# Storing dV and dK from the ScalarE queue, one head later, instead of from the GpSimd queue

## The chip, the cores and the metric

One core of a Trainium2 chip runs the whole kernel. The metric is the device time of that core in microseconds (us), as a median over several executions. Every profile quoted here is of one execution. Two executions of one kernel on different chips or in different rounds differ by up to 0.9% (1738.99 to 1753.90 us for the kernel before), so small differences are judged by ratios against the kernel before, run in the same rounds on the same chip.

## The reference

The program is forward and backward of one decode step: layer norm, attention of one query row against a cache of 4096 keys (4 batches, 32 heads, head size 128), layer norm, SwiGLU. What matters here is the size of two gradients, those of the two caches:

```python
k_cache, v_cache: [4, 32, 4096, 128] bf16          # 128 heads of 1 MB each
dV[b, h] = outer(p, dO)                            # p: [4096], dO: [128]
dP       = V @ dO
dS       = p * (dP - c) * scale
dK[b, h] = outer(dS, q)
```

Each is an outer product, trivial to compute, and 134 MB to write.

## The kernel before

A first loop over 128 heads reads K and V (268 MB). A middle part does the small matrices. The second loop, which the change touches, reads V again (1 MB a head), transposes it on TensorE, computes dP, and builds dV (`gv`) and dK (`gk`) on VectorE, 1 MB each, which are then stored.

All large tiles live in 22 slots of one pool. `give()` puts a slot at the end of a queue of free slots; a later tile takes the oldest, and its writer waits until the slot's last user (often a store) is done.

```python
def front(s):                       # one head ahead of back()
    ...                             # now and then: replicate rows (ScalarE copies)
    V_T(s, psT)                     # PE transposes V; 4 ScalarE copies of 128x1024 to VT
    ...                             # 32 matmuls: dP_ps
    VTs.pop(s).give()
    ...                             # P2: a small copy on GpSimd

def back(s):
    gv = Slot("gv")
    outer(gv.heads(), P2, reps["rdo", ...])                           # VectorE
    nc.gpsimd.dma_start(out=rows_of(out_3[b, h]), in_=gv.heads())     # store dV
    gv.give()
    ...                                                               # dS on VectorE
    gk = Slot("gk")
    outer(gk.heads(), dS2, reps["rq", ...])                           # VectorE
    nc.gpsimd.dma_start(out=rows_of(out_2[b, h]), in_=gk.heads())     # store dK
    gk.give()

def prefetch(s):
    while nv["next"] < min(NH, s + 7) and len(free) > 5:
        load_V2()                   # SP issues the load of a later V

prefetch(0)
front(0)
for s in range(NH):
    prefetch(s + 1)
    ...
    front(s + 1)
    back(s)
    step("s", ...)                  # a piece of side work: weight gradients, dx, ...
```

## Time and profile before

| | before |
|---|---|
| time, median of the runs before the prediction | 1743.91 us (1738.99 to 1747.68) |
| DMA bytes | 707.86 MB, mean 406 GB/s |
| busy share of the span: PE, DVE, ACT, POOL | 76%, 72%, 55%, 28% |
| second loop | about 720 us to the end |

The prediction shows the lines and how they are read. Its DMA row gives the busy share of the 16 DMA engines in tenths, for 40 equal slices of the span.

### The profile page before, as it was taken

What the parts mean: (1) busy time and instruction counts of PE and PEld (TensorE: products, weight loads), DVE (VectorE), ACT (ScalarE), POOL (GpSimd) and SP (SyncE); (2) the same over time, 40 slices, a digit from 0 to 9 for tenths busy, and PEclk for the clock granted to TensorE, in tenths of its full rate; (3) what the DMA queues carried; (4) which work ended last, traced back from release to release, by engine and by line L of the source; (5) the groups of instructions that cost most, each with busy time, mean ns of one, the idle gap of its engine ahead of it and who ended that gap; (6) DMA issues with size and microseconds to landing.
All of it is one profiled execution on the core that took longest, in us unless ns stands there. A gap on an engine that the chain in (4) does not pass through costs nothing.

```text
span 1743.7 us, 44065 instructions
## 1 busy us (share of the span) xinstructions
PE 1324.2 (76%) x18993; PEld 1122.6 (64%) x18993; DVE 1251.9 (72%) x1382; ACT 956.4 (55%) x1463; POOL 491.6 (28%) x804
## 2 busy tenths in 40 slices
PE   5889888888888888888877876676667766786653
PEld 4777766666666667878777875565446555665553
DVE  5899899899898996567746765647545555655674
ACT  3455445445444444665555655575566666766653
POOL 2333333333333331213321331212212212322332
PEclk8999999999999999755555555666556555656555
DMA  9999999999999999899999999999999999999997
GB/s 397 410 418 419 419 418 419 419 416 418 410 413 397 418 405 362 320 403 411 423 418 419 417 417 417 417 420 387 423 412 403 415 420 393 386 415 412 416 415 301
DMA packets 107124, 707.86 MB, mean 406 GB/s; under 512 B 11233, under 2 KB 18921, under 8 KB 23985
## 3 DMA queue, kind: packets, MB, share of 16 engines
q1 hardware_dynamic: 67280, 422.68, 59.5%
q0 software_dynamic: 39648, 282.36, 39.3%
q8 instruction: 149, 2.44, 0.5%
q14 instruction: 47, 0.38, 0.1%
HBM read 422.58 MB, written 282.34 MB: 404 GB/s over the span
## 4 chain that ended last, share of the span: by engine, by line
DMA 38%; DVE 11%; issue 6%; PE 4%; ACT 2%; POOL 1%; DVEq 0%; POOLq 0%; ACTq 0%; SPq 0%
DMA out_dram<-gk 21%; DMA out_dram<-gv 11%; DVE gk L1077 4%; DVE gv L1077 4%; DMA out_dram<-gw 4%; DMA out_dram<-gwq 1%; ACT VT L740 1%; POOL P L1073 1%; DMA V<-in_A_v_cache_dram 1%; PE pt_tps L739 1%; PE M_ps L436 1%; DVE PK L421 1%; ACT wo L216 0%; DVE dS L1095 0%; PE pt_w L564 0%
## 5 line engine op out<-in xcount | busy, mean ns | idle before, releaser
L740 ACT COPY VT<-pt_tps 128x1024 bf16<-128x1024 bf16 x512 | 492.8, 1015 | 286.9 <-PE pt_tps L739 121.8
L739 PE MATMUL pt_tps<-ident_b,V 128*128 128x128 bf16 x4096 | 457.7, 296 | 168.3 <-ACT VT L740 165.1
L739 PEld LDWEIGHTS <-V 128*128 128x128 bf16 x4096 | 407.0, 139 | 237.2 <-issue 224.7
L1077 DVE TENSOR_TENSOR gv<-P,reps 128x4096 bf16<-128x4096 bf16 x128 | 293.0, 2289 | 256.4 <-DMA out_dram<-gk 145.6
L1077 DVE TENSOR_TENSOR gk<-dS,reps 128x4096 bf16<-128x4096 bf16 x128 | 293.4, 2292 | 76.7 <-DMA out_dram<-gv 34.9
L421 DVE TENSOR_TENSOR PK<-Kn,PK 128x4096 bf16<-128x4096 bf16 x128 | 302.9, 2367 | 36.4 <-POOL PK L417 36.4
L436 PE MATMUL M_ps<-PK,Vn 128*128 128x130 bf16 x4096 | 287.2, 223 | 43.2 <-DMA Vn<-in_A_v_cache_dram 43.0
L436 PEld LDWEIGHTS <-Vn 128*128 128x128 bf16 x4096 | 254.3, 99 | 63.1 <-DMA Vn<-in_A_v_cache_dram 53.6
L328 DVE STREAM_TRANSPOSE KT<-Kn 128x512 f32<-128x512 f32 (+1 forms) x321 | 251.0, 798 | 0.5 <-issue 0.5
L323 ACT COPY KT<-pt_tps 128x1024 bf16<-128x1024 bf16 x128 | 129.5, 1012 | 190.1 <-PE pt_tps L322 157.9
L1070 PE MATMUL dP_ps<-dOT_bf,VT 128*128 128x1 bf16 x4096 | 151.5, 166 | 72.7 <-ACT VT L740 62.7
L1070 PEld LDWEIGHTS <-VT 128*128 128x128 bf16 x4096 | 141.6, 104 | 84.6 <-ACT VT L740 73.9
L1099 POOL DMA_DIRECT2D out_dram<-gk x128 | 68.4, 534 | 383.7 <-DVE gk L1077 369.1
L1089 POOL DMA_DIRECT2D out_dram<-gv x128 | 68.7, 537 | 351.4 <-DVE dSt L1092 340.6
L417 POOL COPY PK<-P_all 128x64 bf16<-128x64 bf16 x128 | 32.5, 254 | 437.9 <-ACT P_all L411 432.6
L336 POOL COPY zq<-qT_bf 128x2 bf16<-128x2 bf16 x128 | 152.3, 1190 | 0.0
L1073 POOL COPY P<-P_all 128x64 bf16<-128x64 bf16 x128 | 121.5, 949 | 0.0
L411 ACT COPY P_all<-pt_P 32x64 bf16<-32x64 bf16 x256 | 52.1, 203 | 58.2 <-PE pt_P L407 56.0
L322 PE MATMUL pt_tps<-ident_b,Kn 128*128 128x128 bf16 x1024 | 80.5, 223 | 0.7 <-DVE qrep L282 0.7
L446 PE MATMUL kP_ps<-PK,onesw 128*32 128x512 bf16 x1024 | 80.1, 389 | 0.0
L322 PEld LDWEIGHTS <-Kn 128*128 128x128 bf16 x1024 | 62.1, 100 | 26.3 <-issue 26.3
L400 ACT ACTIVATE Pn<-E,rl 128x1024 bf16<-128x1024 f32 x64 | 73.7, 1151 | 2.8 <-DVE rl L397 2.8
(234 smaller groups left out, 1298.2 us busy)
## 6 DMA issues: line engine op xcount, KB each, us to landing
Kn<-in_A_k_cache_dram SPq DMA_DIRECT2D x128, 1024.0 KB, 14.3
Vn<-in_A_v_cache_dram SPq DMA_DIRECT2D x128, 1024.0 KB, 15.1
V<-in_A_v_cache_dram SPq DMA_DIRECT2D x128, 1024.0 KB, 11.4
out_dram<-gv POOLq DMA_DIRECT2D x128, 1024.0 KB, 19.3
out_dram<-gk POOLq DMA_DIRECT2D x128, 1024.0 KB, 19.8
wq<-in_A_wq_dram SPq DMA_DIRECT2D x8, 1024.0 KB, 11.2
out_dram<-gw POOLq DMA_DIRECT2D x6, 896.0 KB, 21.9
wo<-in_A_wo_dram SPq DMA_DIRECT2D x4, 1024.0 KB, 11.1
```

What stands on the lines that cost most here:

```text
L322: nc.tensor.transpose(pt[:, i, :], Kn[:, c * GW + i, :], ident_b[:])
L323: nc.scalar.copy(out=KT[:, c * GW:(c + 1) * GW, :], in_=pt[:])
L328: nc.vector.transpose(out=KT[:, c * w_:(c + n) * w_], in_=Kn[:, c * w_:(c + n) * w_])
L336: nc.gpsimd.tensor_copy(out=zq[gi % 2][hl][:, 32:132:67], in_=qT_bf[:, s:s + 1].to_broadcast([P, 2]))
L421: nc.vector.tensor_tensor(out=PK[:, :, 0:Dh].rearrange("p j (r t) -> p j r t", t=2), in0=Ks[s].heads().rearrange("p j (r t) -> p j r t", t=2),
L436: nc.tensor.matmul(hold["M"][:], lhsT=Vn[:, j, :], rhs=PK[:, j, :], start=(j == 0), stop=(j == SJ - 1))
L446: nc.tensor.matmul(hold["kP"][32 * q:32 * (q + 1), :, :], lhsT=ones_window(w), rhs=PK[:, j0:j0 + 4, 0:Dh], start=(w == 0 and c == 0), stop ...
L739: nc.tensor.transpose(pt[:, i, :], Vn[:, g * GW + i, :], ident_b[:])
L740: nc.scalar.copy(out=VT[:, g * GW:(g + 1) * GW, :], in_=pt[:])
L1070: nc.tensor.matmul(dP_ps[:, j:j + 1], lhsT=VT[:, j, :], rhs=dOT_bf[:, s:s + 1], start=True, stop=True)
L1073: nc.gpsimd.tensor_copy(out=P2[:], in_=P_all[:, s, :, None].to_broadcast([P, SJ, 2]))
L1077: nc.vector.tensor_tensor(out=dst.rearrange("p j (r t) -> p j r t", t=2), in0=col2[:, :, None, :].to_broadcast([P, SJ, Dh // 2, 2]), in1=r ...
```

## The change

Its intent is to take the stores' issue off GpSimd, and to keep ScalarE, which runs its instructions in order, from waiting for VectorE: the store of head s-1 is put behind ScalarE's copies for head s+1, when its data has long been made.

```diff
             outer(gv.heads(), P2, reps["rdo", s // REP][:, s % REP, :])
-            nc.gpsimd.dma_start(out=rows_of(out_3[b, h]), in_=gv.heads())
-            gv.give()
 ...
             outer(gk.heads(), dS2, reps["rq", s // REP][:, s % REP, :])
-            nc.gpsimd.dma_start(out=rows_of(out_2[b, h]), in_=gk.heads())
-            gk.give()
+            late.append((b, h, gv, gk))
+
+        late = deque()
+
+        def store_late():
+            b, h, gv, gk = late.popleft()
+            for out_ap, sl in ((out_3, gv), (out_2, gk)):
+                nc.scalar.dma_start(out=rows_of(out_ap[b, h]), in_=sl.heads())
+                sl.give()
 ...
                 front(s + 1)
+            if late:
+                store_late()
             back(s)
             step("s", 1 if s < 44 else 2 + (s % 4 == 0))
+        store_late()
         step("s", 400)
```

## The prediction

> **What bounds the kernel now.** I read the page's slices first, then the queue table, the windows of 50 us, and the chain of waits. The slices:
>
> ```profile
> DMA  9999999999999999899999999999999999999997
> GB/s 397 410 418 419 419 418 419 419 416 418 410 413 397 418 405 362 320 403 411 423 418 419 417 417 417 417 420 387 423 412 403 415 420 393 386 415 412 416 415 301
> ...
> q1 hardware_dynamic: 67280, 422.68, 59.5%
> q0 software_dynamic: 39648, 282.36, 39.3%
> ```
>
> The 16 DMA engines are busy in every slice but the seventeenth and the last, at 410 to 420 GB/s. The two queues fill 98.8% of their time. Both queues cost alike: 59.5/422.68 = 0.141% a MB for loads through the hardware queue, 39.3/282.36 = 0.139% for stores through the software queue; in the packet records an 8 KB packet takes 309 ns at the median in both. 707.86 MB at the 419 GB/s of the best long stretch is 1689 us, so whatever a change does to queues can gain at most 55 us (3.1%), and only where the engines are not yet full. The windows (us; busy us of PE, PEld, DVE, ACT, POOL; clock; DMA share; GB/s) say where that is:
>
> ```profile
> 720.00:725.00 5.00, 3.99 (x69) 3.57 (x67) 1.66 (x3) 3.85 (x4) 0.63 (x1) 0.80 0.51 206
> 725.00:730.00 5.00, 3.48 (x61) 3.12 (x58) 4.66 (x4) 3.76 (x4) 2.25 (x2) 0.88 0.30 126
> 730.00:735.00 5.00, 4.70 (x59) 4.45 (x58) 4.88 (x4) 3.36 (x4) 2.53 (x4) 0.50 0.95 387
> ...
> 950.00:1000.00 50.00, 42.75 (x529) 40.21 (x528) 38.41 (x32) 30.77 (x34) 16.91 (x24) 0.57 1.01 418
> ...
> 1500.00:1550.00 50.00, 41.44 (x526) 34.39 (x524) 37.36 (x31) 37.80 (x48) 18.62 (x23) 0.57 0.96 386
> ...
> 1728.00:1730.00 2.00, 0.00 (x0) 0.00 (x0) 0.00 (x0) 0.00 (x0) 0.00 (x0) 0.50 0.91 381
> ...
> 1732.00:1734.00 2.00, 0.00 (x0) 0.00 (x0) 0.00 (x0) 0.00 (x0) 0.00 (x0) 0.50 0.13 53
> ...
> 1738.00:1740.00 2.00, 0.00 (x0) 0.00 (x0) 0.00 (x0) 0.00 (x0) 0.00 (x0) 0.50 0.05 20
> ```
>
> The stage that the change touches, the second loop over 128 heads, runs from about 720 us to the end, at a share of 1.01 nearly throughout. It isn't full at its start (720 to 730), where few transfers are ready, a little around 1500, and in the last 8 us, where a share of 0.05 to 0.13 means that one or two of 16 engines still drain. The waits (us in total, times, longest) agree:
>
> ```profile
> DVE gv L1077 <- DMA out_dram<-gk: 145.6, 38, 9.9
> ...
> ACT VT L740 <- DMA out_dram<-gk: 64.7, 16, 12.4
> DVE gv L1077 <- DMA out_dram<-gv: 63.4, 22, 7.8
> ```
>
> The page's costliest groups and its table of issues have the stores themselves:
>
> ```profile
> L1089 POOL DMA_DIRECT2D out_dram<-gv x128 | 68.7, 537 | 351.4 <-DVE dSt L1092 340.6
> ...
> out_dram<-gk POOLq DMA_DIRECT2D x128, 1024.0 KB, 19.8
> ```
>
> VectorE and ScalarE wait for slots that a store still holds. A store of 1 MB lands 19.8 us after its issue, though at 419 GB/s it needs 2.5 us alone: it stands behind some seven others. So these waits are back-pressure of full DMA engines, not the cost of issuing. A head has 3 x 1.049 = 3.15 MB, 7.6 us at 415 GB/s (8.0 us with the weights and their gradients, estimated from the stage: (1743.7 - 720)/128); its other work is shorter: VectorE 2.29 + 2.29 + 0.25 + 0.23 = 5.1 us, ScalarE 4 x 1.015 + 0.3 = 4.4 us.
>
> **What the Trainium skill says.** Page "DMA: Bandwidth & Descriptors", section "Issuing engines are not separate DMA queues": transfers from the scalar, sync and gpsimd engines run on the same 16 engines and interleave, and several issuers save only issue time. The trace agrees (0.141 against 0.139% a MB). Same page, "SWDGE vs HWDGE vs iDMA": GpSimd's descriptors are built by software into rings in SBUF, from which VectorE can lock it out; transfers of SP and ACT are immune. The trace shows GpSimd's small copy of P at 0.25 us in places and 1.48 us beside VectorE's long multiply, but its issue at a steady 0.53 us, so I see no cost in the issue. Same page, "Latency and other measured facts": DMA engines 7 and 15 are usually slower, perhaps for the software rings. The trace does not name engines, but a transfer's completion semaphore rises 16 times, once per engine: for stores late in the kernel (1550 to 1700 us) the 16th rise comes 6 to 8 us after the 15th, for loads within 0.5 us. One engine lags in the software queue.
>
> **The change, part by part.**
> 1. Issue leaves GpSimd: 128 x (537 + 534 ns) = 137 us of 492 busy. GpSimd is idle 72% of the span, so nothing on the path: 0 us.
> 2. Issue comes to ScalarE. A 1 MB load takes SP 0.33 us to issue (the trace, typical); I take that for ACT: 2 x 0.33 = 0.66 us a head, 84 us in all. ScalarE goes from 4.4 to 5.0 us a head against 8.0 us: hidden, 0 us. The built program puts the two stores after the four VT copies of the head after next; their data was made an iteration before, so ScalarE rarely waits for VectorE.
> 3. The slots are held one head longer. I listed the slot order of both programs: before, a gv most often takes the slot of the gk stored three iterations before; after, gk most often takes that of a gv whose store is issued two iterations before, for the same head, three back. Loads still run seven heads ahead. So a cycle of three heads, 3 x 8.0 = 24 us, has to hold a store's flight, 2.3 us of multiply and up to one ScalarE turn of 5 us. That leaves some 17 us; the shortest flight of a store in 1000 to 1300 us was 9.2 us, with loads beside it. DMA stays full.
> 4. A new coupling: before, SP's loads have eight completion semaphores and GpSimd's stores eight more. In the changed program loads and stores share eight in rotation: each transfer must wait for the one eight places earlier, a store for one some three heads back. Eight MB in flight is 8.4/0.415 = 20 us of work. That is enough to keep the engines full, and the slot of point 3 waits for a younger store, so it binds first: I take 0 us in the plain stretch and +3 us where side work (small transfers, 1050, 1200, 1500 us) breaks the order.
> 5. The start. Before, stores 0 are issued at 721.6 and 727.8 us. After, both follow ScalarE's copies for head 2, which ended at 735.5. In 720 to 735 the engines moved 5 x (206 + 126 + 387) = 3.6 MB; with under 1 MB of late loads taken off, about 2.8 MB of stores move later: 2.8/0.415 = 7 us, and DMA time lost in a full stage does not come back: +7 us.
> 6. The end. The lagging engine drains alone for some 8 us. If hardware descriptors make it as even as loads are, part of that goes. Loads of the first loop still show two halves of engines 2 to 5 us apart, so I take half: -4 us. The last stores are issued 2.5 us or so later at most, behind a backlog of 20 us: 0.
> Sum: 1743.9 + 7 + 3 - 4 = 1749.9 us.
>
> **Rivals.** *(a) ScalarE becomes the bottleneck*: its order now ties copies, gradient evacuation and stores together; a store that waits for its semaphore stops the copies, PE, and dP. For it: ACT is 76% busy in 1500 to 1550, and one SP issue behind many small packets took 14 us. Against: 3 us spare a head, and older stores than those VectorE waits for. If 3 us in a third of the heads were lost: +120 us, 1870; half a us a head: +64 us. *(b) The software queue is the hidden brake*: rings and the lagging engine cost rate all along, and the store's wait for its slowest engine is what VectorE waits for. For it: the lag of 6 to 8 us of a 19 us flight. Against: the share is 1.01 and packets cost 309 ns in both queues, so the other engines weren't idle for it. At most the 55 us above; I'd expect 15 to 25 if true, 1720 to 1730. *(c) Nothing moves*: start and end cancel, 1740 to 1746.
>
> **Range and chances.** Runs of before span 1739 to 1748. Rival (c) and my sum lie within 10 us; (b) pulls down by 20, the mild form of (a) up by 25: 1732 to 1775. Over 2% faster (under 1709) needs nearly all of the 55 us: 0.04. Over 2% slower (above 1779) needs the strong form of (a), which I can't exclude as the coupling is new: 0.12. Within: 0.84.
>
> **What would show it.** Right: DMA share 1.01 at about 415 GB/s between 750 and 1700; an empty stretch of DMA until about 735 us; ScalarE's issue near 0.33 us; waits of VectorE for stores much as before; a shorter thin tail with the 16th rise close to the 15th. Wrong: DMA shares under 0.97 over long stretches, with ScalarE waiting for stores or loads just ahead of its issue (a), or above 420 GB/s throughout (b); an issue on ScalarE that lasts microseconds would sink point 2, loads landing much later than 11 us point 4.

## The result, and the profile after

The changed kernel takes 1748.82 us (median of six runs, 1746.28 to 1750.50); the kernel before took 1745.8 us with the new runs added (six, 1738.99 to 1748.95). The ratio is 1.002 with a 95% interval of 0.9997 to 1.0043: the same, perhaps slower by 3 us. Ratios here are the mean time of one kernel's fast runs over that of the other's of the same rounds, so they aren't quite the ratio of the quoted medians. A second job gave 1.0042 (1.0030 to 1.0055): on that chip the changed kernel is slower by 7 us.

From the page of the changed kernel, the DMA rows, the queues, and the two stores among the issues (KB each, median us from issue to landing):

```profile
DMA  9999999999999999599999999999999999999998
GB/s 398 410 418 418 419 418 418 419 413 418 417 415 398 418 406 360 245 397 412 423 419 397 423 419 414 409 397 387 425 425 415 414 412 410 414 419 415 418 424 337
...
q1 hardware_dynamic: 67280, 422.68, 59.5%
q10 hardware_dynamic: 36864, 268.45, 37.2%
q0 software_dynamic: 2784, 13.91, 2.0%
...
out_dram<-gv ACTq DMA_DIRECT2D x128, 1024.0 KB, 12.7
out_dram<-gk ACTq DMA_DIRECT2D x128, 1024.0 KB, 15.2
```

The stores have moved to a queue of their own, q10, and cost there what they did in q0: 37.2/268.45 = 0.139% of the engines' time for each MB. The DMA row is as full as before, with two differences: the seventeenth slice, the start of the second loop, falls from 8 to 5 tenths and from 320 to 245 GB/s, and the last one rises from 7 to 8. The stores land in 13 to 15 us instead of 19 to 20, so less stands in front of them, but that speeds nothing: the engines had work either way.

The windows of the start and of the end, from the changed kernel (us; busy us of PE, PEld, DVE, ACT, POOL; clock; DMA share; GB/s):

```profile
715.00:720.00 5.00, 3.99 (x33) 3.36 (x31) 2.58 (x2) 3.06 (x5) 3.41 (x5) 0.50 0.42 172
720.00:725.00 5.00, 4.29 (x63) 3.98 (x61) 1.79 (x3) 3.48 (x5) 0.00 (x0) 0.50 0.01 3
725.00:730.00 5.00, 4.36 (x70) 4.08 (x70) 4.05 (x5) 3.17 (x4) 0.24 (x1) 0.84 0.00 0
730.00:735.00 5.00, 3.93 (x55) 3.66 (x53) 2.66 (x2) 3.49 (x4) 0.00 (x0) 0.50 0.33 133
735.00:740.00 5.00, 4.65 (x58) 4.34 (x58) 4.83 (x5) 3.52 (x4) 0.24 (x1) 0.50 0.70 290
...
1736.00:1738.00 2.00, 0.00 (x0) 0.00 (x0) 0.00 (x0) 0.00 (x0) 0.00 (x0) 0.50 0.16 66
1738.00:1740.00 2.00, 0.00 (x0) 0.00 (x0) 0.00 (x0) 0.00 (x0) 0.00 (x0) 0.50 0.06 25
1740.00:1742.00 2.00, 0.00 (x0) 0.00 (x0) 0.00 (x0) 0.00 (x0) 0.00 (x0) 0.50 0.07 29
```

From 720 to 730 us the DMA engines do next to nothing, and from 715 to 740 they are never full. The end still has its thin tail: one of 16 engines (a share of 0.06) drains alone for several microseconds, although no large store goes through the software queue any more.

ScalarE's issues in order of time show why the start is empty. It is the timeline of ScalarE in the changed kernel (start, us, instruction; in brackets the idle time before and its releaser):

```profile
729.64 1.93 ACT L740 COPY VT<-pt_tps 128x1024 bf16<-128x1024 bf16 x2 [1.64 <-PE pt_tps L739]
731.75 1.93 ACT L740 COPY VT<-pt_tps 128x1024 bf16<-128x1024 bf16 x2 [0.18 <-PE pt_tps L739]
732.72 0.37 ACTq L1105 DMA_DIRECT2D out_dram<-gv  x1
733.19 0.38 ACTq L1105 DMA_DIRECT2D out_dram<-gk  x1
736.29 1.93 ACT L740 COPY VT<-pt_tps 128x1024 bf16<-128x1024 bf16 x2 [2.62 <-PE pt_tps L739]
738.41 1.93 ACT L740 COPY VT<-pt_tps 128x1024 bf16<-128x1024 bf16 x2 [0.19 <-PE pt_tps L739]
739.38 0.34 ACTq L1105 DMA_DIRECT2D out_dram<-gv  x1
```

The first stores leave behind the copies of head 2, at 732.7 us, though VectorE had made the first gv by 719.7; before the change they left at 721.5 and 727.7. The next pair follows one turn of ScalarE later, 6.7 us after the first.

**A ledger of idle time.** To add up where time went I summed the packet records of each trace: for a stretch, its length less the sum of its packets' times over 16. Records overlap a little (hence shares of 1.01), so a full stretch comes out slightly negative; only differences count. "Packets" is the sum of all packet times over 16, "end" is the time from the last packet to the end of the span. Each row adds up to its span. The lines r1 to r10 belong to the experiments below; r10 and r1 are second traces of the kernel before and of the changed one.

```
us              0-715  715-760  760-1040  1040-1600  1600-1720  1720-last  packets   end    span
before           -1.9     6.4     -2.9      -1.8       -1.4        7.7     1733.6    4.1   1743.7
before (r10)     -3.4     8.9     -2.7       0.2       -1.4        7.4     1732.3    4.1   1745.5
changed          -4.0    17.9     -1.7      -4.7       -0.8        6.2     1730.2    1.5   1744.6
changed (r1)     -3.5    18.4     -2.7      -1.9       -0.9        6.1     1731.0    1.5   1747.9
r2 late, GpSimd  -2.6     8.9     -3.1      -6.0       -1.4        9.8     1727.7    4.1   1737.4
r3 at once, ACT  -3.8    10.0     -2.4       3.8       -1.4        2.7     1728.5    1.5   1738.9
r4 first 3 once  -3.1    13.3     -2.8      -3.1       -0.8        5.2     1735.9    1.4   1746.0
r5 switch at 24  -3.2     6.8     -3.1      -2.0       -0.3        5.4     1731.5    1.5   1736.6
r6 two late      -3.1    24.2     -2.5      -1.0       -1.2        2.4     1731.8    1.5   1752.0
r7 early V       -3.6    13.3      5.5      -2.2       -1.4        4.6     1737.3    1.4   1754.9
r8 early V, Gp   -3.0     9.6     -2.4      -6.0       -1.4        9.4     1727.7    4.1   1738.1
r9 before copies -3.0    12.0     -2.4       2.6       -0.6        3.2     1730.6    1.4   1743.9
```

Two traces of one kernel agree within 1 to 3 us in each column. With the means of both traces, the change adds 10.5 us at the start (7.65 to 18.15) and takes away 2.5 in the stretch with side work, 1.4 in the tail, 2.4 in packet time, 2.6 at the end and 1.1 ahead of the stage (which is scatter, the program is the same there); it adds about 0.6 in each of the two other stretches. The sum is +1.7 us, the difference of the spans of these traces. The term of the side work is no larger than the scatter between two traces of one kernel there (2.0 and 2.8 us), so that part of what gives time back is not sure.

### The profile page after: what moved, and what is told of

Same layout as the page of the kernel before. It is cut to its first block, busy times and chain, and to the rows that moved or that the text cites. A ratio compares the mean times of both kernels' runs of the same rounds, so it can differ in the third digit from the quotient of the medians.

```text
span 1744.6 us, 43821 instructions
## 1 busy us (share of the span) xinstructions
PE 1316.6 (75%) x18993; PEld 1106.4 (63%) x18993; DVE 1253.4 (72%) x1382; ACT 956.8 (55%) x1463; POOL 291.2 (17%) x548
## 3 DMA queue, kind: packets, MB, share of 16 engines
q10 hardware_dynamic: 36864, 268.45, 37.2%
## 4 chain that ended last, share of the span: by engine, by line
DMA 34%; PE 10%; ACT 9%; DVE 6%; issue 3%; ACTq 1%; SPq 0%; POOL 0%; DVEq 0%
DMA out_dram<-gv 13%; DMA out_dram<-gk 10%; ACT VT L740 8%; DMA V<-in_A_v_cache_dram 7%; PE pt_tps L739 4%; DVE gv L1077 3%; DVE gk L1077 1%; DMA wq<-in_A_wq_dram 1%; PE dq_ps L902 1%; DMA w2a<-in_B_w_dram 1%; DMA w<-in_B_w_dram 1%; ACTq L1105 1%; PE dP_ps L1070 1%; DMA wo<-in_A_wo_dram 1%; PE rep_ps L1054 1%
## 5 line engine op out<-in xcount | busy, mean ns | idle before, releaser
L739 PE MATMUL pt_tps<-ident_b,V 128*128 128x128 bf16 x4096 | 446.1, 290 | 96.9 <-ACT VT L740 96.9
L739 PEld LDWEIGHTS <-V 128*128 128x128 bf16 x4096 | 396.2, 137 | 184.1 <-issue 176.6
L1073 POOL COPY P<-P_all 128x64 bf16<-128x64 bf16 x128 | 57.7, 466 | 587.0 <-DVE gv L1077 587.0
L1090 DVE TENSOR_SCALAR dSt<-dP_ps,c_rep 128x32 f32<-128x32 f32 x128 | 31.6, 247 | 79.2 <-PE dP_ps L1070 79.0
L1057 ACT CAST reps<-rep_ps 128x512 bf16<-128x512 f32 x64 | 37.4, 585 | 69.4 <-PE rep_ps L1054 50.6
```

The source lines that it names most:

```text
L739: nc.tensor.transpose(pt[:, i, :], Vn[:, g * GW + i, :], ident_b[:])
```

## The experiments

Theory S: the start alone costs, because ScalarE's place in the order delays the first stores while the DMA engines have nothing else; the rest gives a little back. Rival A: ScalarE becomes the bound. Rival C: the eight completion semaphores, which loads and stores now share, cost time. Rival N: there is no difference at all.

**r1, the changed kernel again** (no edit), in one job with r2, r3 and r4.

> The changed kernel once more, as the base for the other three on this chip. Its trace has no DMA traffic from 717 to 732 us, and is 4.5 MB further behind the kernel before at 760 us than at 715 us (10.9 us at 415 GB/s), of which it wins back 2.5 MB between 1400 and 1700 us. Theory S (start): it is 3 us slower because the start loses 9 to 11 us and the later part gives 5 or 6 back. Theory N (noise): no difference, ratio 1.000. Expected: ratio to before 1.0015 to 1.003, again an empty stretch of about 15 us at the start, and a thin tail of 6 to 8 us at the end.

Measured: 1749.74 us, ratio 1.0042 (1.0030 to 1.0055), a bit over the expected range. The hole at the start is there again (18.4 us idle), and the thin tail lasts 7.0 us. Rival N falls.

**r2, only the lateness.** The stores stay on GpSimd.

```diff
-                nc.scalar.dma_start(out=rows_of(out_ap[b, h]), in_=sl.heads())
+                nc.gpsimd.dma_start(out=rows_of(out_ap[b, h]), in_=sl.heads())
```

> Only the lateness: the stores are issued one head later, but still from GpSimd, with their own eight semaphores. Theory S: the empty stretch at the start is a thing of the lateness alone, so it is here too, 12 to 16 us long, and the time is that of before plus 6 to 10 us (ratio 1.004 to 1.006) if what the changed kernel wins back later comes from the queue, or that of the changed kernel (1.002) if it comes from the lateness. Rival C (the shared eight semaphores cost time): this one is faster than the changed kernel by 3 us or more.

Measured: 1738.73 us, ratio 0.9974 (0.9961 to 0.9986), faster than both kernels. My expectation of an empty start was wrong, and the windows of r2 say why:

```profile
720.00:725.00 5.00, 4.22 (x63) 3.91 (x61) 1.68 (x1) 4.11 (x5) 2.39 (x2) 0.50 0.38 154
725.00:730.00 5.00, 4.22 (x58) 3.91 (x54) 3.80 (x4) 3.85 (x4) 0.79 (x2) 0.63 0.28 111
730.00:735.00 5.00, 4.25 (x67) 4.07 (x68) 3.94 (x4) 3.19 (x4) 1.18 (x3) 0.71 0.89 362
```

The first stores of r2 leave at 722.0 and 728.3 us, hardly later than before the change. "One head later" is a place in the program, and on GpSimd little stands ahead of that place: a small copy of P. On ScalarE four copies of 1 us stand there, which wait for TensorE. So lateness in the program is late in time only on a busy queue. By itself r2 fits rival C too (11 us faster than the changed kernel), so the next runs had to decide.

**r3, only the queue.** The stores are issued from ScalarE in `back`, right behind their multiply.

```diff
-            nc.gpsimd.dma_start(out=rows_of(out_3[b, h]), in_=gv.heads())
+            nc.scalar.dma_start(out=rows_of(out_3[b, h]), in_=gv.heads())
 ...
-            nc.gpsimd.dma_start(out=rows_of(out_2[b, h]), in_=gk.heads())
+            nc.scalar.dma_start(out=rows_of(out_2[b, h]), in_=gk.heads())
```

> Only the queue: each store is issued from ScalarE right after its multiply, so ScalarE waits for VectorE in every head. Theory S: the DMA engines have work sooner, the empty stretch at the start shrinks to under 8 us, and the middle stays full (share 1.01) because ScalarE has 3 us to spare a head: 1740 to 1748 us. Rival A (ScalarE's order becomes the bound when it waits for VectorE): copies for the next head start only after gk, the cycle of a head rises above 8 us, DMA share falls under 0.97 in the middle, and the time is over 1780 us.

Measured: 1740.96 us, ratio 0.9994 (0.9981 to 1.0007): the time of the kernel before. The start is idle for 10.0 us, a little more than the 8 us I had set. Rival A falls: even with each store right behind its multiply in ScalarE's order the middle stays full (-2.4 from 760 to 1040 us). The waiting shows only beside side work, where the idle time is 3.8 us against -1.9 and -4.7 of the changed kernel. That is what the lateness was for, and it is worth about 7 us there; at the start it costs about 8 us. These two nearly cancel. That r3 is still faster than the changed kernel comes from its shorter tail (2.7 us against 6.2 and 6.1) and 2 us less packet time, which no experiment here explains.

**r4, the first three heads at once.** As in the changed kernel, but for s < 3 both stores are issued from GpSimd in `back`.

```diff
+            if s < 3:
+                nc.gpsimd.dma_start(out=rows_of(out_3[b, h]), in_=gv.heads())
+                gv.give()
 ...
-            late.append((b, h, gv, gk))
+            if s < 3:
+                nc.gpsimd.dma_start(out=rows_of(out_2[b, h]), in_=gk.heads())
+                gk.give()
+            else:
+                late.append((b, h, gv, gk))
```

> The changed kernel, but the stores of the first three heads go out at once from GpSimd, as before the change. Theory S: the start is as full as before, and the kernel is 8 to 11 us faster than the changed kernel: 1737 to 1741 us, ratio to before 0.996 to 0.998. Rival (the start doesn't matter, a full DMA makes up for it later): the same time as the changed kernel within 3 us.

Measured: 1746.86 us, ratio 1.0022 (1.0008 to 1.0035), 3 us below r1 where I expected 8 to 11. That number is within what the rival foresaw, but the windows of r4 show that the hole moved:

```profile
730.00:735.00 5.00, 3.81 (x62) 3.53 (x59) 4.88 (x5) 3.85 (x4) 2.53 (x3) 0.57 0.79 321
...
740.00:745.00 5.00, 3.84 (x50) 3.60 (x48) 3.60 (x4) 2.10 (x4) 1.13 (x2) 0.50 0.96 387
745.00:750.00 5.00, 4.19 (x63) 3.81 (x61) 2.54 (x2) 3.85 (x4) 0.24 (x1) 0.73 0.40 121
750.00:755.00 5.00, 3.81 (x60) 3.54 (x59) 3.52 (x3) 3.86 (x4) 0.00 (x0) 0.62 0.48 203
```

Up to 745 us the engines are about as busy as before the change. Then head 3, the first late one, leaves a gap of 745 to 755 us, since its stores have to wait for a turn of ScalarE. The ledger has 5 us less idle time in this stretch than in the changed kernel, but also 5 us more packet time for the same bytes (1735.9 us), which nothing here explains; so the time of r4 alone decides nothing. I read from the windows that the start as such is not what costs, but the beginning of ScalarE's lateness, wherever the DMA engines have no backlog at that moment. I call that theory S2. If instead the toll of one turn has to be paid wherever the lateness begins (rival T), no placement helps.

**r5, switch at head 24.** Late stores for all heads, from GpSimd for the first 24 heads and from ScalarE from then on.

```diff
-            late.append((b, h, gv, gk))
+            late.append((s, b, h, gv, gk))
 ...
-            b, h, gv, gk = late.popleft()
+            s, b, h, gv, gk = late.popleft()
+            q = nc.gpsimd if s < 24 else nc.scalar
 ...
-                nc.scalar.dma_start(out=rows_of(out_ap[b, h]), in_=sl.heads())
+                q.dma_start(out=rows_of(out_ap[b, h]), in_=sl.heads())
```

> Late stores in all heads, but from GpSimd for the first 24 heads and from ScalarE from then on. r2 (late, GpSimd) had no empty start (715 to 760 us: 8.9 us of idle against 17.9 and 18.4 of the changed kernel and 6.4 before). r4 (first 3 heads at once) filled the start but lost 1.7 MB between 740 and 750 us, where ScalarE's lateness began. Theory S2: the lateness behind ScalarE's copies costs once, where it begins, only if the DMA engines have no backlog then; at head 24 they have one, so nothing is lost: idle of 715 to 760 us as in r2, and 1738 to 1742 us, 7 to 11 us below the changed kernel. Rival T (the toll of one head is paid wherever ScalarE's lateness begins): an idle stretch of 4 us or more around 900 us, and 1745 us or more.

Measured: 1739.42 us, ratio 0.9960 (0.9937 to 0.9983). The start is idle for 6.8 us, and around the switch nothing is lost; r5's windows of both:

```profile
720.00:725.00 5.00, 4.27 (x64) 4.03 (x63) 2.53 (x3) 3.66 (x4) 0.00 (x0) 0.50 0.53 213
725.00:730.00 5.00, 3.73 (x66) 3.46 (x65) 3.87 (x5) 3.18 (x5) 1.32 (x3) 0.84 0.55 224
730.00:735.00 5.00, 4.51 (x60) 4.36 (x60) 2.86 (x2) 2.74 (x3) 0.77 (x2) 0.50 0.97 385
...
880.00:900.00 20.00, 17.24 (x205) 16.14 (x205) 15.96 (x13) 12.62 (x14) 6.36 (x9) 0.50 1.01 424
900.00:920.00 20.00, 16.06 (x191) 15.08 (x192) 16.36 (x16) 11.20 (x14) 0.94 (x4) 0.59 1.01 416
920.00:940.00 20.00, 10.66 (x132) 10.11 (x131) 14.08 (x10) 6.71 (x8) 0.71 (x3) 0.50 1.01 421
```

The fifth busy column (POOL) falls from 6.36 to 0.94 us: there, from 900 us on, the stores change over, at a DMA share of 1.01. Rival T falls. Rival C falls too: 104 of 128 heads in r5 store from ScalarE, share the eight semaphores with the loads, and the kernel is as fast as r2, which doesn't share them. With r2 this is the fastest version; both beat the kernel before by 0.3 to 0.4%.

**r6, two heads late.** The suspected cost doubled.

```diff
-            if late:
+            if len(late) > 1:
                 store_late()
 ...
-        store_late()
+        while late:
+            store_late()
```

> The suspected cost doubled: ScalarE stores two heads late. Theory S2: the first store is issued one turn of ScalarE later, at about 739 instead of 732.7 us, so the idle of 715 to 760 us grows from 18 to 23 to 25 us and the time by 5 to 7 us over the changed kernel (ratio to before 1.006 to 1.008), with DMA share 1.01 from 800 us on. Rival B (the slots: four held instead of two leave too few stores in flight): share below 0.98 in the middle, and over 1765 us.

Measured: 1761.29 us, ratio 1.0075 (1.0049 to 1.0102). (The kernel before took 1747.7 us in this job, a slower one than in the others.) The first store leaves at 738.6 us, the start is idle for 24.2 us, and from 760 to 1040 us the engines are full (-2.5). By the ratios this is 6 to 10 us above the changed kernel (1.002 and 1.0042). The first store and the idle time are as S2 had them, the time a little over. The ledger's trace is of the fastest of the six executions (1753.77 us), and where the other 7 us of the median went is open. Rival B falls for the plain stretch, where holding four slots instead of two starves nothing. At the start it has a part: nearly all that r6 is idle beyond the changed kernel falls between 735 and 760 us, where its loads move 0.35 MB instead of 2.1. Its eleventh V load leaves at 756.6 us, when the store of head 2's gv has landed, against 743.3 us; so late stores delay loads too.

**r7, loads into the hole.** The changed kernel, with V loads allowed sooner in the first heads.

```diff
-            while nv["next"] < min(NH, s + 7) and len(free) > 5:
+            while nv["next"] < min(NH, s + (12 if s < 8 else 7)) and len(free) > (2 if s < 8 else 5):
```

> The changed kernel with V loads of later heads allowed sooner during the first eight heads (up to 12 heads ahead, down to 2 free slots), so that two more loads of 1 MB can run in the empty stretch. Theory S2: DMA time lost in the empty stretch is what costs; 2 MB moved there save 2.1/0.415 = 5 us: 4 to 6 us below the changed kernel. Rival: the later part is not bound by DMA, so no gain (within 2 us).

Measured: 1753.81 us, ratio 1.0040 (1.0012 to 1.0068). My expectation failed in the time, not in the hole: the start is idle for 13.3 instead of 18 us, as two more loads would give, but from 760 to 1040 us 5.5 us are lost where the changed kernel lost none (-1.7 and -2.7). In time the rival's forecast (no gain) came true, but not for its reason: the hole moved, it was not filled. The trace of r7 shows how. The first gv now waits until head 0's dP matmuls have freed a slot, and starts at 723.3 us instead of 717.4; a copy of ScalarE waits 10.2 us for the slot of a gk, until 775.3; and from 780 to 800 us the V loads move 0.1 MB where they moved 3.3 in the changed kernel. Whether taken slots or the limit's return to seven heads at head 8 stops the loads there was not tested. The packets also take 7 us more in sum (1737.3 us), unexplained.

**r8, the same on r2.**

> Late stores from GpSimd (r2, the fastest so far: 0.9974 of before) with the same early V loads. Theory S2: the empty stretch of r2 is smaller but there, two loads fit in, 3 to 5 us below r2: ratio to before 0.994 to 0.996, faster than both kernels. Rival: the loads only displace the first stores, same as r2 within 2 us.

Measured: 1739.59 us, ratio 0.9965 (0.9942 to 0.9988), no better than r2. The start is idle for 9.6 us: the loads took slots from the first stores (the first gv is begun at 724.4 us instead of 719.4, and its store leaves at 727.0 instead of 722.0). The rival written beside it was right.

**r9, the stores ahead of the copies.** As changed, but `store_late()` stands before `front(s + 1)`.

```diff
             prefetch(s + 1)
+            if late:
+                store_late()
 ...
                 front(s + 1)
-            if late:
-                store_late()
```

> The changed kernel with its two stores moved ahead of the VT copies of the next head in ScalarE's order: slots are still held until the next iteration, the semaphores are still shared, but the store isn't behind ScalarE's copies. Theory S2 (the place behind the copies empties the start): store 0 leaves at about 728 us instead of 732.7, the idle of 715 to 760 us falls from 18 to 10 to 12 us, and the time is 5 to 8 us below the changed kernel. Rival C2 (holding the slots and sharing the semaphores are what costs): no gain, 1747 us or more. If holding the slots is also what removes the idle time of 1500 to 1600 us (1.6 before and 1.3 in r3, which doesn't hold them; -1.1 to -1.2 in the kernels that do), it is gone here too.

Measured: 1745.73 us, ratio 1.0021 (0.9994 to 1.0048); the chip scatters much in this job (1743.58 to 1756.06). The first store leaves at 725.5 us and the start is idle for 12.0 us, as expected. The expected gain in time did not come: by the ratios it is nothing to 4 us (1.0021 against 1.002 and 1.0042), by the spans of the traces 0.7 and 4.0. In the ledger 2.6 us are idle beside side work, as in r3, which takes back most of what the start gains. So r9 confirms S2 in where the start's idle time comes from, but its time doesn't decide between S2 and rival C2. Both kernels make ScalarE stop for VectorE. My side guess, that holding the slots removes the idle time of 1500 to 1600 us, isn't borne out: r9 holds them and has 0.8 us there.

**r10, the kernel before again.**

> The kernel before once more, for a second trace: how far the terms read from one trace repeat. Theory S2 needs the idle of 715 to 760 us to be near 6 us again (within 2), that of 1500 to 1600 near 1.6, the thin tail 6 to 11 us, and some 4 us between the last packet and the end. If they scatter by more than 3 us, the ledger can't be read to that accuracy.

Measured: 1744.58 us, ratio 1.0003. Its row in the ledger agrees with the first trace within 3 us in every column. The start, 8.9 us against 6.4, is a little outside the 2 us I had set, so a single trace's start is good to some 3 us.

## Why the prediction was right or wrong

The time was predicted at 1750 us and measured at 1748.8 (1749.7 in the second job). The bound and the mechanism were right; several terms of the sum were mis-sized, and one had the wrong sign. That the sum came so near is partly luck: the start was set 3.5 us too low and side work 5.5 us too high, and these errors cancel.

- **What bounds the kernel: right.** In the plain stretch from 760 to 1040 us the engines stay full in every experiment but r7, and of the kernels that only move the stores, by ratio, the one with more idle time at the start is the slower one: r5 and r2 (7 and 9 us), r3 (10), r9 (12), r4 (13), the changed kernel (18), r6 (24). The kernel before is the exception: 6.4 and 8.9 us, yet slower than r5 and r2. One reading was too smooth: the row isn't at 410 to 420 GB/s in all slices but two, it has 362 to 405 in several that are marked nine.
- **Issue leaves GpSimd, 0 us: right.** POOL falls from 491.6 to 291.2 us of busy time and nothing follows from it. 137 us of that are the issues; its copies of P also take 57.7 instead of 121.5 us in all.
- **Issue comes to ScalarE, 84 us in all and hidden: hidden, but too small.** In the trace of the changed kernel the 256 issues take 131 us: 0.34 us at the median, but 37 of them over 1 us (up to 1.76), in all 47 us. The middle is full all the same.
- **The slots, 0 us: right but for the start (see there).** VectorE's waits for stores didn't grow. The two lines answer to those shown of before (us in total, times, longest):

```profile
DVE gv L1077 <- DMA out_dram<-gk: 93.0, 20, 13.2
...
DVE gv L1077 <- DMA out_dram<-gv: 53.3, 15, 8.9
```

- **Shared semaphores and side work, +3 us: wrong sign.** The stretch from 1040 to 1600 us lost 2.5 us less than before the change, by the mean of two traces each. The coupling does exist. ScalarE's waits in the changed kernel name loads of V that its next gradient copy has no use for, and no such wait stands in the traces of before, r2 and r8, whose stores GpSimd issues; I read this as the copy standing behind a store that waited for its semaphore's last owner:

```profile
ACT gw L889 <- DMA V<-in_A_v_cache_dram: 23.8, 11, 3.3
...
ACT gwq L889 <- DMA V<-in_A_v_cache_dram: 11.5, 3, 7.4
ACT gwo L889 <- DMA V<-in_A_v_cache_dram: 11.5, 4, 4.7
```

  These 46.8 us must be mostly hidden, since the DMA engines are nearly full in this stretch. r3 and r9 show, in one trace each, what the lateness is good for when ScalarE issues the stores: without it, or ahead of the copies, 2.6 to 3.8 us are idle in this stretch, with it -1.9 to -4.7.
- **The start, +7 us: right in kind, too small.** It measured +10.5 us. The first store left at 732.7 us where I had 735.5. But I took off late loads that weren't there (0.1 MB after 720 us, not nearly 1), and counted only the bytes of 720 to 735 us. By the means of two traces each, the changed kernel moves 3.1 MB less in that time and 0.8 MB less from 735 to 760: 3.9 MB, not 2.8, or 9.4 us at 0.415 MB a us. (The rest of the 10.5 is 0.5 MB of loads that ended on the other side of 715 us.) What is missing after 735 us is loads, not stores: stores move 6.6 MB there against 6.2 before, V loads 2.1 against 3.3. The eleventh V load leaves at 743.3 us, when the store of head 1's gv has landed; before it left at 736.0. In r2, where the same store leaves early, it leaves at 736.4. So the late store empties the start twice: by itself, and by the slot that a load waits for, which my point 3 had at no cost.
- **The end, -4 us: the size was right, the reason mostly not.** The tail gives 1.4 us; the other 2.6 us come from something I hadn't seen, the time between the last packet and the end of the span: 4.1 us before, 1.5 after. In it a DRAIN instruction of GpSimd at the program's end, 21 to 22 us long, is over only 2.95 us after the last rise of a completion semaphore, in each of the four traces whose last stores GpSimd issued; in the other eight no DRAIN of GpSimd after that rise lasts over 0.1 us. The lag of one engine was to go with the software queue. For stores from 1500 to 1600 us it is smaller (the 16th rise of a completion semaphore comes 3.3 and 3.4 us after the 15th, at the median of the two traces; 5.8 and 7.2 before), but in the last 50 us it is 5.8 and 4.8 us, with the stores on a hardware queue alone. Nor does that queue bring it about: in r3 and r9, on the same queue, it is 0.6 and 1.0 us there, and their tails are 2.7 and 3.2 us. What sets it is open.
- **Rivals.** (a) has no support in r3, which gives ScalarE the worst order and costs nothing in sum, though a few us beside side work. (b) was nearer than I thought: r2, r5 and r8 are 0.3 to 0.4% faster than before. But the queue is not the reason, for r2 and r8 use the software queue for every store. Two things differ in the ledger of r2 and r8: less idle time beside side work (-6.0 against -1.8 and 0.2) and 1727.7 us of packet time against 1733.6 and 1732.3 for the same bytes. Why packets of the same sizes take 5 us less in sum isn't settled.

## What to carry to other kernels

Where the DMA engines are full, moving a store to another queue changes nothing by itself; look for the places where they aren't, here the first microseconds of the stage and its last, and ask what the change does there. "One iteration later" on an in-order engine means "behind all that this engine does in that iteration": free on an idle queue, one turn of the loop on a busy one, and it costs only if it begins when there is no backlog. So keep the early stores on a queue with nothing in front of them and switch once the backlog stands, as r5 did. In r7, a hole filled with loads that take the stores' buffers only moved.

## What the Trainium skill lacked or had wrong

- "DMA: Bandwidth & Descriptors", section "Issuing engines are not separate DMA queues", says that several issuers save only issue time. Packet cost agrees (0.139% of the engines' time a MB in either store queue). What it lacks is that the issuer's place in the order can empty the DMA engines at the start of a stage: 18 us of idle time against 6 to 9 with the same transfers.
- The same page, section "Latency and other measured facts", ties the slower engines to the software rings, as a guess. Here the 16th rise of a store's completion semaphore came 5.8 us after the 15th in the last 50 us of the changed kernel, whose large stores all use a hardware queue, and 0.6 us in r3, on the same queue. The trace doesn't name the engine, so it is open whether it is one of the two that the page names.
- No page that I read has the time from the last packet to the end of the program: 4.1 us in the four traces whose last stores GpSimd had issued, with a DRAIN of GpSimd that ends 2.95 us after the last landing, and 1.4 to 1.5 us in the eight where ScalarE had.
- No page that I read says how far an issue on ScalarE or SP can stretch on this chip. In the changed kernel ScalarE's took 0.34 us at the median, over 1 us in 37 of 256, 1.76 at most; in the kernel before, an SP issue of a load took up to 13.96 us, behind loads cut into 1 KB packets.
